# Attention and maxout FFN on one core: the ninth key blocks of four heads in 64x64 tiles of the array, 114 tiles masked on VectorE, the order of the work made anew

## The chip, the core and the metric

One core of a Trainium2 chip runs the whole program. Its engines work side by side, each through its own queue in order: TensorE (PE, with its weight loads shown apart as PEld), VectorE (DVE), ScalarE (ACT), GpSimd (POOL) and SyncE (SP), which here issues nearly all transfers. The metric is the time of one execution on the device, in microseconds; lower is better.

## The reference

Eight batches of eight heads, 576 positions of 64 numbers each. Attention keeps only scores within tau of the row's largest; its output goes through a feed-forward net with three parallel layers.

```python
scores = scale * np.matmul(q, k.transpose(0, 1, 3, 2))
thresh = np.max(scores, axis=-1, keepdims=True) - tau
scores = np.where(scores >= thresh, scores, -1000000000.0)
...
attn = attn / (np.sum(attn, axis=-1, keepdims=True) + 1e-09)
attn_out = np.matmul(attn, v)
...
h = np.maximum(np.maximum(x @ w1, x @ w2), x @ w3)      # x: 4608 x 512, w: 512 x 768
return h @ w_out                                        # 768 x 512
```

## The kernel before

**Tiling.** Four heads of one batch are a quad; there are 16 quads, two to a batch. The 576 positions are 9 blocks of 64 per head; two heads share the 128 partitions, so that a quad has two pairs of heads, r = 0 and 1 below. A chunk is 128 query rows of a quad, a tile is a chunk's scores for one r, 128 x 576 in fp32. A quad has 9 chunks and 18 tiles; there are 288 tiles.

**One tile.** `scores` (L287) makes it on TensorE in fp32 in a PSUM slot of two banks; there are four slots (SLOTS). The matmuls work in halves of the array: 64 rows x 128 columns (64\*128 in the profile's rows), and the ninth query chunk in four 64x64 tiles (64\*64). `maximum` (L319) takes the row maximum on VectorE. Then there are two ways, by a string of 288 digits, MASKED (L24), read by `masked` (L311). A tile with 0: ScalarE subtracts and flattens (`exponents`, L331, Prelu out of PSUM), then takes the exponential and its row sum (`numerators`, L339). A tile with 1: VectorE writes the negated scores to SBUF with the maximum, ScalarE takes one exponential, VectorE compares with the threshold, multiplies and sums in one instruction (SCALAR_TENSOR_TENSOR). So a masked tile uses ScalarE once and VectorE twice, one that isn't uses ScalarE twice and VectorE once.

After both tiles of a chunk, VectorE takes reciprocals (`reciprocals`), GpSimd scales to bf16 (`normalized`, tile P), and a transfer on SyncE's queue transposes P into `ptq` (`turned`).

**The product with V.** `product` (L366) multiplies a pair of heads' transposed probabilities by V in bf16 with 128 rows and 64 columns of the array (128\*64), two column tiles at once for the two heads of the pair. The 576 keys are four blocks of 128 and a ninth one of 64. The ninth blocks of the two pairs share one 128-row slot of `ptq` (index 4), pair 0 in rows 0 to 63 and pair 1 in rows 64 to 127. V for it is padded: three tiles `vr` are zeroed once in the other pair's rows (memsets, L553), and `cast_v` copies the 64 rows of each pair in, one GpSimd instruction for each. So the ninth block takes a whole pass of 128 rows for each product, of which half are zeros. The result is copied out of PSUM to `xt` by VectorE for pair 0 (`on_vector`) and by ScalarE for pair 1 (`on_scalar`).

**FFN.** `ffn` (L432): 18 hidden pieces (`hid`) a batch on TensorE, combined by ScalarE (copy, `hm`) and VectorE (two maxima), then output pieces (`outp`, `ninth`), copied out by ScalarE and stored. The last batch is split in two parts (SPLIT) of 256 and 320 positions, so that its first part can be worked on earlier.

**The order.** Every engine runs its instructions in the order of one string, ORDER (L40): each letter issues one step, and `_Ordered` (L82) chains each engine's instructions in that order. S, T, O, F, B are steps of TensorE (scores, transposes of q and k, products, first and second halves of FFN pieces; the digit names the PSUM slot); m, k, r, c, v, w are VectorE's; e, n, a, h, u, x ScalarE's; p, q, y, z GpSimd's (scaling, swapped copies of q, casts of V, casts of weights); l, t, g, o SyncE's transfers (loads, transposes of P, weights, stores). An engine doesn't step over an instruction that waits.

Of the kernel before, what the change touches and what calls it, by code (L numbers as in the profile page):

```python
# [12 lines left out]
BF16 = mybir.dt.bfloat16  # L13
# [11 lines left out]
010100101001000000011101001010000001100010001000101000011000100000100000  # L25
000011111001100001001001001001000001011100101001000110001010010000010011
000010011101100001001100100001001010001100010111000001000100000110000101
001001001101100000110001000100100100001100100011100111010011010111110110
# [12 lines left out]
lllllmlyelgS2ymylS3emgnlT0mleS1lakS2nlqermS3ylmeS0pmeS1kpS3elmS2nlzmelrmnT1pS0tcnperkT1pameS1zmteS3knpS0rnmp  # L41
emS2permeqS1mnqT3meqktepS0ncS2ntrpmS3npretprmeS1pmnS0tpmS3npmS1etpmeS0rT2mnplkeT1akgeS2qmgepmteS3rkpekntS0pe
rrnmT2pncS3ptamepS1meqtrS2meyqnS3lmqeS0pmelpknT1lpS2nmeymeS3lrkepS0tcnT2rpnmS1tpnmaprrmS0eS2pmteS1pmT3epctep
meT3O0ykntnyS2etrykpnO1wnprmaS0xptrS3meS2zmeS1mzgeS0mlnS3pmleS1pmelO2qmelpkteO0nrnklpS3nlwgxprrmS2leS0pmeF3q
tmT1eBqcF0eqkthBpnS2vS1nF3pmnF0pmBerBkepS2vhT1tnprmS0S3apmetS1zmeS2rmpeF3tmF0epBkepF1tnBvBznvS2ghS3rymnF0gmS
1eplBrkepF2tnmF3BnpvBnqvT1S0hprrcT2S3pamS1eymzF2emBeqgkF0etyS3nS1vpnmtF2pBmezBveS3prgnS0mtS1phrmT3epO2metzeF
0wpnS1gcqS2nmBqnmO3zekepgS1xvlF2nS3mtnF0rrmpBeBlpveS1lphS2mntF3zmeBrpS0evS1lpnmF2lnpS3rmleBptmS1nzvS0nS3mtpn
S2rpeF1rmepmtepS0mBepmtekF3ektekT2uBarklpukS0uqlS2urS1mlnS3pmleO0pmlepmelO2wtnkS1xrS0tepmF2myF3eBkepT1tBhcF0
nqvT2T1laByrcynS3qvS2nlqmF1tnpF0meS3pBelmBlhrrF2kpelS1vnBlprF3mnlS0pveBtprmS1hS2pmeS3tpmeS0pmF2emF1eBkeT3Bva
tF0nvqT2T3BkqlaS1nrcS3phmtS2npmF0epF1mteBqkBeqF3lnvS2lnBrvplS0hmtpS1F3meS2mteBrmepS0vnpO1rekpnO3mtnpweS2yrrt  # L50
xS1mF0yymT3epBcnS1pvS2nptF3meS0pmeBomT2hS1okeF0omF3ntBkaBervS1ponrF2vpemS0ptuS3mpeF2metknT1T3rknBparrceS0puS
3mqtuS1mpeS2mpeS3lmF0peomepS1ketqT3S2ncBqnmlqnmlO3ekluktO1urnwperrS0pxS3mptnS2mS1pempS3etmF0peF2meBlkBelS1kh
oF3nrmlF0pnBtvpBerrvS2phlS1mnpS3tmF0peS2mpeBmeF3vF1eoBkntS0vnBS2rmhpS3mepS1mteyF2mF0eyBkteBnrvT3pF1aovT2ynBp
lrcS3hplS0mnyF2lmF1elBykepBlnvT3tS0aS2vnO3rrmtpnmpeS1weptS2mS0prmO3eqtmeqF1eqlT0S2xqcBnlpmS3hlpS0meF2ymF1elB
knlF3vnBokBetS2hvS0nrrF3mpF1mpeBkBpetF2vnprS0uvnT3ptmS2aS1pmeS0trmF3epmnpkeS2tS0ermpBnmopnkS1uS2rurompS0eF3o
mpelmpeS2lkpeS0lmS1elqBmelqmetkO2unktO0erwpurkpT1txT2cS3apF0nmtT1qS2ceBqmnS1yF3hmF2eyrBpeBvptnF0pS1vnBrmtpS3
hS2pmeS0mtS1eF3meF2meBkBeF0knF1vnBBrvhpS3nvT0pF2akyF1tnBmyS0velByrmlS3phS2rlempF1lmyeF0pklBepS3tnvS2nBrmptO1
meprvepS2wnS3plmF0nF1rmepBlkeqS2lBhmtT3nyS0vnS2mqlO1emtpecT2xT0rS3pacF1eqmF2lnyBklqeT0BvlaS3khoS1qnmF0tF2pme
BrBopnvS3teprvF0pnrmS1puS2meS3prmS0epF1tmepmepT2ktBeqncT3tuS0kaS2urqmS3tnpmS1nF0pmemteS3repS1mS2lepmBelykteS
3kuO1rumplnmlpO0ewterpT2xS1cqnoS3mpF0nF2metBkeBkF1hlF3nvBlnrrS0pvlnBpmS2lhS1ymleF0mtS3epBmepF2vF1etkBnS0vnS3  # L60
rmBnpS2rhmpF0emF1pteBkpBerF3vnS2ptvnT0pBramS1pthS0mepF3meqtT2rBecpS1nvylT0ynS2pmlS3amlS1eomS0elO2rmpeomeplO3
ketnwT1F0nctF2xkBnBrvpS1hrF3pmS0qBemqS2onvF1yeF0mBopkeF3tyBnS2vqhBrlrnmpT1S0vaptS2empF1S3mpelBkeplF0vntS2rum
S1pnS0mtepF3rmepmetqS2kS0epBnmmteS1rkepS2lmuS0ulpmS1nlymT3yetF2cekeT3oBrknpamoS0npS3mnS1qtmuO0qurrmqelO2wpel
kpelS0xS3meptF2mS1peBemytF0hrkT3pBecF2nS1vpnS3rymtBpnmS0epS1vlnF3mF2etBmeBkhF0lkeF3nBrvpS1nrvBpnS2mptS0hmpeS
3meF2tmF1eBkeBlrvnT0plS3ravlpS2nlmqF0nlS1mqeBtrrmpF2eS3phBlmepS0tvepS1mS2npS3mepO0meknO1meownT3orxkT2pS0tacF
1nF2qrmeBtpS3evpBmS0tyhF1meT2yBcqoeF3rpkT2F0aptBnvBnS2pvS1hqtmF3nqT0meBrS1npvF2npmT3BactS1ervF3prmS0pueS2omp
F3ekqelmT1ntS0qcnBpmekteS2S1urrmpF0uompekS3eptS2nmS1pnmlO3ermtpekO2pnwS1ykxtyS3emS2BomeyrmepS1rukpS2uoF3meF0
opmnBtykBhpS1ervS2eptmO3pO0mxnS3txS2rmepF0empF1ekBtBevF3hkS2nS0mnBrmF1npF2vepBkBtS0hvO3emO2xkS1xerS3rpmF2mpF
0eF1kpteBnBvpF3BvtBrhkpF2S0vS1prmBptmF3eF0pveBtBhS1vS2mS3mF0F1mBkBF2vhF3keBeO0vnO1kF2kxeBwurS1rvpS0mpS2F3mpe
tmpeS0eoF1mnketBknkBurrupoF2puF0hptF3uvF2pvF1hF0tvF3rvpF2hF1vopF0vF3thF2vF1vF0hoF3vF2ovF1hF0vF3vO2uoO1wF0xF3  # L70
F2hF1vF3vF2hF1vF3vF2hF1vF3vF2hF1vF3vF2hF1vF3vF2hF1vBvF3uuooBF2uuuooo
# [31 lines left out]
def kernel(  # L103
# [609 lines left out]
    x = 0  # L713
# [39 lines left out]
```

## Time and profile before

| | us |
|---|---|
| timed runs, median of 3 | 447.21 |
| lowest and highest | 446.19, 447.46 |
| profiled execution, first to last instruction (span) | 445.0 |
| transposes of P, 144 on SyncE's queue, median to landing | 4.1 |
| loads of V, 32 of 256 KB, median to landing | 5.1 |

The profile shows one execution. Its page has busy times of each engine, busy tenths in 40 slices, the chain of work that ended last, and groups of instructions. All of the kernel's instructions are recorded at line 91, in the helper that keeps the order, so that they are told apart by the names of their tiles: sc are scores, o products with V, ph hidden pieces, po output pieces, tp transposes. A matmul's duration includes the time that it takes to run through, and the next one begins before it ends; so starts are compared, not durations. An fp32 matmul shows as two passes. TensorE ran at its full granted clock from 60 us on (mean 0.94 before that).

### The profile page before, as it was taken

To read this page: it belongs to the slowest core of one execution; us is meant where nothing else is said; L and a number is where in the kernel's file an instruction comes from. 1 tells how busy PE (TensorE), PEld (TensorE's weight loads), DVE (VectorE), ACT (ScalarE), POOL (GpSimd) and SP (SyncE) were. 2 spreads that over 40 slices of the span, in tenths; PEclk is the share of its full clock that TensorE was granted. 3 is DMA by queue.
4 is the path that set the end of the run, shared out by engine and by line. 5 is a ranking of instruction groups with operands and counts; after the bars stand their busy time and mean duration, and the time that the engine had idled before them with its cause. 6 is when DMAs were issued, how large, how long until landed. Compare 5 with 4: busy or idle time off the path is not lost.

```text
span 445.0 us, 14089 instructions
## 1 busy us (share of the span) xinstructions
PE 423.6 (95%) x5193; PEld 313.3 (70%) x5193; DVE 393.2 (88%) x1093; ACT 394.4 (89%) x804; POOL 315.9 (71%) x422
## 2 busy tenths in 40 slices
PE   7767799999999999999999999999999999999995
PEld 5434557767787767777687867867687778777772
DVE  4989889999999999989989998999999999989641
ACT  4999999999999999999998999999999999956422
POOL 3998989989686686686768885859767789562300
PEclk9998899999999999999999999999999999999999
DMA  8989999999999978999797999899999979882902
GB/s 251 331 162 213 243 195 234 221 245 229 215 255 195 250 165 175 234 187 228 179 223 170 200 224 182 211 234 199 197 220 202 253 121 173 148 122 34 217 13 108
DMA packets 212773, 87.44 MB, mean 196 GB/s; under 512 B 185824, under 2 KB 199648, under 8 KB 212704
## 3 DMA queue, kind: packets, MB, share of 16 engines
q1 hardware_dynamic: 212000, 85.69, 93.6%
q10 hardware_dynamic: 704, 0.85, 0.6%
q8 instruction: 41, 0.67, 0.6%
q14 instruction: 28, 0.23, 0.2%
HBM read 34.60 MB, written 9.44 MB: 99 GB/s over the span
## 4 chain that ended last, share of the span: by engine, by line
PE 81%; ACT 7%; DVE 6%; issue 4%; POOL 2%; DMA 1%; DVEq 0%; POOLq 0%; ACTq 0%
PE ph L91 30%; PE sc L91 28%; PE po L91 11%; PE o L91 8%; ACT z L91 6%; PE tp L91 4%; DVE z L91 2%; DVE unused L91 2%; DMA qm<-in_q_dram 1%; POOL P L91 1%; DVE hm L91 0%; POOL w L91 0%; ACT qt L91 0%; POOL qs L91 0%; DVE hT L91 0%
## 5 line engine op out<-in xcount | busy, mean ns | idle before, releaser
L91 POOL TENSOR_SCALAR P<-z,rs 128x576 bf16<-128x576 f32 x288 | 228.1, 807 | 85.7 <-DVE rs L91 36.4
L91 PE MATMUL sc<-kt,qt 64*128 64x320 f32 (+2 forms) x640 | 179.1, 429 | 4.9 <-ACT z L91 4.4
L91 PE MATMUL sc<-kt,qs 64*128 64x256 f32 (+2 forms) x640 | 178.6, 418 | 4.7 <-ACT z L91 2.7
L91 PE MATMUL ph<-xt,w 64*128 64x288 bf16 (+2 forms) x2160 | 163.9, 283 | 0.3
L91 PEld LDWEIGHTS <-w 64*128 64x128 bf16 (+1 forms) x2160 | 124.8, 94 | 30.9 <-issue 5.3
L91 DVE TENSOR_SCALAR_CACHE_REDUCE unused<-sc 128x576 bf16<-128x576 f32 x183 | 133.2, 749 | 8.9 <-PE sc L91 8.4
L91 ACT ACTIVATE z<-sc,nm 128x576 f32<-128x576 f32 x183 | 131.3, 740 | 8.5 <-DVE unused L91 5.2
L91 ACT ACTIVATE z<-z 128x576 f32<-128x576 f32 x183 | 123.5, 680 | 0.1
L91 PEld LDWEIGHTS sc<-kt,qs 64*128 64x128 f32 (+1 forms) x640 | 92.4, 178 | 25.3 <-ACT z L91 8.1
L91 PEld LDWEIGHTS sc<-kt,qt 64*128 64x128 f32 (+1 forms) x640 | 92.4, 178 | 19.8 <-ACT z L91 9.3
L91 DVE SCALAR_TENSOR_TENSOR z<-z 128x576 f32<-128x576 f32 x105 | 84.1, 811 | 0.4 <-ACT z L91 0.4
L91 DVE TENSOR_SCALAR_CACHE_REDUCE z<-sc 128x576 f32<-128x576 f32 x105 | 77.7, 752 | 7.4 <-PE sc L91 3.4
L91 ACT ACTIVATE z<-z,nm 128x576 f32<-128x576 f32 x105 | 79.1, 773 | 3.6 <-DVE z L91 3.2
L91 POOL COPY qs<-qt 64x640 f32<-64x640 f32 (+3 forms) x68 | 47.0, 692 | 14.4 <-ACT qt L91 11.0
L91 PE MATMUL po<-wo,hT 64*128 64x512 bf16 (+1 forms) x480 | 54.0, 356 | 0.1
L91 DVE TENSOR_TENSOR hm<-ph,hm 128x576 bf16<-128x576 f32 (+2 forms) x54 | 37.0, 686 | 13.0 <-PE ph L91 11.8
L91 ACT ACTIVATE hm<-ph 128x576 bf16<-128x576 f32 (+2 forms) x54 | 32.1, 594 | 18.4 <-PE ph L91 18.1
L91 PEld LDWEIGHTS <-hT 64*128 64x128 bf16 (+1 forms) x480 | 29.6, 97 | 17.1 <-issue 2.9
L91 DVE TENSOR_TENSOR hT<-ph,hm 128x576 bf16<-128x576 f32 (+2 forms) x54 | 37.2, 688 | 3.1 <-PE ph L91 0.6
L91 PE MATMUL o<-ptq,vb 128*64 128x64 bf16 (+2 forms) x544 | 38.7, 282 | 0.0
L91 ACT ACTIVATION_READ_ACCUMULATOR z<-z 128x1 f32 x183 | 36.2, 198 | 0.0
L91 PEld LDWEIGHTS <-vb 128*64 128x64 bf16 x544 | 22.6, 111 | 15.1 <-issue 6.8
(32 smaller groups left out, 274.2 us busy)
## 6 DMA issues: line engine op xcount, KB each, us to landing
vm<-in_v_dram SPq DMA_DIRECT2D x32, 256.0 KB, 5.1
out_dram<-ob SPq DMA_DIRECT2D x31, 256.0 KB, 2.8
qm<-in_q_dram SPq DMA_DIRECT2D x15, 512.0 KB, 4.5
km<-in_k_dram SPq DMA_DIRECT2D x15, 512.0 KB, 5.4
stage<-in_moe_w_dram SPq DMA_DIRECT2D x9, 512.0 KB, 5.3
ptq<-P SPq DMA_TRANSPOSE x144, 4.1
stage<-in_moe_w_out_dram SPq DMA_DIRECT2D x3, 512.0 KB, 4.7
qm<-in_q_dram SPq DMA_DIRECT2D x16, 64.0 KB, 2.9
```

What stands on the lines that cost most here:

```text
L91: ins = fn(*a, **kw)
```

## The change

- The ninth key blocks leave `product`, which now has four blocks. A new step N follows every second product: for both pairs of heads of the quad, the ninth block is multiplied with 64 rows and 64 columns of the array (`ninths`), pair 0 in the upper rows, pair 1 in the lower, two heads each in columns, and added to what the two products left in PSUM. The copies to `xt` (w, x) can be issued only after N.
- V for the ninth block is no longer padded: the six memsets go, the three fixed tiles are replaced by a pool tile `vrb` of 128 rows, and one GpSimd copy takes the place of two.
- In the last batch's second part the product's columns now lie at 256 to 575 of the bank, not at 0 to 319, so that each part lies in a bank as the others do.
- MASKED is new, with 114 ones in place of 105.
- ORDER is new throughout. It has the same steps, plus 18 N, less 16 y; and 9 k stand in place of 9 n.

```diff
 MASKED = """
-010100101001000000011101001010000001100010001000101000011000100000100000
...
+001110001001001001001000011110010001100000110110001001100000100001100001
...
 ORDER = """
-lllllmlyelgS2ymylS3emgnlT0mleS1lakS2nlqermS3ylmeS0pmeS1kpS3elmS2nlzmelrmnT1pS0tcnperkT1pameS1zmteS3knpS0rnmp
...
+S2ymlmS3lS1lelgllllllmlmlmS0T3mneeknamT2T1S3reeqaS1pqekmkS0enmrS3mcmpnreneS0S2merypenpmS1qnzkS3ppS2pmtS0geeT1
...
-    vrs = [one.tile([128, 4, D], BF16, name=f"vr{x}") for x in range(3)]
...
-        L["vrb"] = vrs[(2 * L["b"] + L["qd"]) % 3]
-        for r in range(2):
-            rows = slice(64 * r, 64 * r + 64)
-            pool.tensor_copy(out=L["vrb"][rows, 2 * r:2 * r + 2], in_=L["vr"][rows])
-            yield
+        L["vrb"] = vp.tile([128, 2, D], BF16, name="vrb")
+        pool.tensor_copy(out=L["vrb"], in_=L["vr"])
+        yield
...
-        order = [(m, run) for m in range(5) for run in runs] if part is None else \
-            [(m, run) for run in runs for m in range(5)]
+        order = [(m, run) for m in range(4) for run in runs] if part is None else \
+            [(m, run) for run in runs for m in range(4)]
...
-                    w = vb[:, 2 * r + i, (1, 3, 0, 2)[m], :] if m < 4 else vrb[:, 2 * r + i, :]
-                    tensor.matmul(ps[64 * i:64 * i + 64, p0:p0 + n], w,
-                                  pt[:, 4 if m == 4 else m + 5 * r, q0[i]:q0[i] + n],
-                                  start=(m == 0), stop=(m == 4))
+                    tensor.matmul(ps[64 * i:64 * i + 64, p0:p0 + n], vb[:, 2 * r + i, (1, 3, 0, 2)[m], :],
+                                  pt[:, m + 5 * r, q0[i]:q0[i] + n], start=(m == 0), stop=False)
+
+        def ninths(run):
+            *q0, p0, n = run
+            rows = slice(64 * r, 64 * r + 64)
+            for i in range(2):
+                tensor.matmul(st["ps"][64 * i:64 * i + 64, p0:p0 + n], vrb[rows, i, :],
+                              pt[rows, 4, q0[i]:q0[i] + n], start=False, stop=True)
...
-    for t in vrs:
-        for x in range(2):
-            vector.memset(t[64 - 64 * x:128 - 64 * x, 2 * x:2 * x + 2, :], 0.0)
...
             p.first(where)
-            for k, fn in (("x", p.scalar), ("w", p.vector)):
-                if fn:
-                    line[k].append(fn)
+            line["N"].append(p)
+        elif what == "N":
+            both = [line["N"].pop(0) for _ in range(2)]
+            for run in both[0].runs:
+                for p in both:
+                    p.ninths(run)
+            for p in both:
+                for k, fn in (("x", p.scalar), ("w", p.vector)):
+                    if fn:
+                        line[k].append(fn)
```

More of the change, by code (lines that the diff above doesn't have):

```diff
@@ L46 @@
[L46 to L60, printed above, removed]
@@ L392, in on_vector @@
             else:
-                vector.tensor_copy(out=dst[:, 256:S], in_=ps[:, 0:320])
+                vector.tensor_copy(out=dst[:, 256:S], in_=ps[:, 256:S])
         def on_scalar():
@@ L402, in on_scalar @@
             else:
-                scalar.activation(out=dst[:, 256:S], in_=ps[:, 0:320], func=AF.Copy)
+                scalar.activation(out=dst[:, 256:S], in_=ps[:, 256:S], func=AF.Copy)
         p = _Piece((L["b"], L["qd"], r, part), first)
@@ L406, in product @@
         p.scalar = on_scalar if part == 1 or r == 1 else None
+        p.runs, p.ninths = runs, ninths
         return p
@@ L595 @@
                 O=products(), F=pieces())
-    line = {k: [] for k in "menkrptahvuxwcq"}
+    line = {k: [] for k in "menkrptahvuxwcqN"}
     casts = iter([w[1] for w in wl])
```

54 lines of the change are left out of this document (35 added, 19 removed).

## The prediction

> **What bounds the kernel now.** I read the page first, its busy line and the chain that ended last.
>
> ```profile
> PE 423.6 (95%) x5193; PEld 313.3 (70%) x5193; DVE 393.2 (88%) x1093; ACT 394.4 (89%) x804; POOL 315.9 (71%) x422
> ...
> PE 81%; ACT 7%; DVE 6%; issue 4%; POOL 2%; DMA 1%; DVEq 0%; POOLq 0%; ACTq 0%
> ```
>
> TensorE carries 81% of the chain; VectorE and ScalarE share 13%. Whole-run shares hide stages, so next came busy time in four stretches, and one slice of 50 us.
>
> ```profile
> core 0: us, PE busy (x) PEld busy (x) DVE busy (x) ACT busy (x) POOL busy (x), PEclk, DMA share, GB/s
> 0.00:60.00 60.00, 43.82 (x389) 28.33 (x393) 48.25 (x145) 52.84 (x110) 49.66 (x72) 0.94 1.04 234
> 60.00:355.00 295.00, 294.30 (x3787) 220.47 (x3780) 278.81 (x772) 284.72 (x579) 226.17 (x301) 1.00 1.04 212
> 355.00:441.00 86.00, 85.53 (x1028) 64.51 (x1024) 66.06 (x178) 56.85 (x116) 40.07 (x51) 1.00 0.62 117
> ```
>
> ```profile
> 200.00:250.00 50.00, 50.00 (x650) 37.89 (x646) 48.06 (x133) 47.47 (x97) 36.47 (x49) 1.00 0.93 194
> ```
>
> Columns: stretch, length, busy us of each engine. Three stages show. Up to 60 us the feed-forward work has hardly begun, TensorE has gaps (43.8 of 60), and ScalarE is fullest (52.8). From 60 to 355 TensorE is busy throughout, yet ScalarE (284.7/295 = 96.5%) and VectorE (94.5%) are nearly as full: a three-way tie. From 355 to 441 only TensorE is full; what is left there is matrix work. Who holds whom in the tie is in the view of waits:
>
> ```profile
> PEld sc L91 <- ACT z L91: 17.3, 31, 2.2
> ...
> DVE unused L91 <- PE sc L91: 8.4, 20, 1.0
> ...
> ACT z L91 <- DVE unused L91: 5.2, 15, 0.7
> ...
> PE tp L91 <- DMA qm<-in_q_dram: 1.1, 2, 0.8
> ```
>
> (us in total, times, longest.) TensorE's score products, first of all their weight loads, wait for ScalarE to release PSUM banks, VectorE's maxima wait for those products, ScalarE waits for the maxima: a ring in which no member waits long. Work taken from TensorE counts fully only after 355, and before that as far as the other two keep up.
>
> **The ninth block.** TensorE around a pair of attention products, by start times (start, duration):
>
> ```profile
> 115.82 0.43 PE L91 MATMUL sc<-kt,qs 64*128 64x320 f32 x1
> 116.18 1.18 PE L91 MATMUL o<-ptq,vb 128*64 128x512 bf16 x16
> 117.19 0.41 PE L91 MATMUL o<-ptq,vr 128*64 128x512 bf16 x4
> 117.44 1.16 PE L91 MATMUL o<-ptq,vb 128*64 128x512 bf16 x16
> 118.43 0.41 PE L91 MATMUL o<-ptq,vr 128*64 128x512 bf16 x4
> 118.78 0.53 PE L91 MATMUL sc<-kt,qt 64*128 64x320 f32 x1
> ...
> 119.15 0.43 PE L91 MATMUL sc<-kt,qt 64*128 64x320 f32 x1
> ...
> 119.42 0.38 PE L91 MATMUL sc<-kt,qt 64*128 64x256 f32 x1
> ...
> 119.63 0.38 PE L91 MATMUL sc<-kt,qt 64*128 64x256 f32 x1
> ```
>
> Durations overlap, so I count from start to start. Four key blocks take 118.43 - 117.44 = 0.99, the fifth (vr, half of it zeros) 117.44 - 117.19 = 0.25. Now the same for the split last batch, and how often each shape runs:
>
> ```profile
> 405.35 0.28 PE L91 MATMUL o<-ptq,vr 128*64 128x256 bf16 x2
> 405.46 0.29 PE L91 MATMUL o<-ptq,vb 128*64 128x64 bf16 x8
> 405.58 0.20 PE L91 MATMUL o<-ptq,vr 128*64 128x64 bf16 x2
> 405.61 0.28 PE L91 MATMUL po<-wo,hT 128*64 128x256 bf16 x2
> ```
>
> ```profile
> L91 PE MATMUL o<-ptq,vr 128*64 128x512 bf16 x56 | 11.4, 382 | 0.0
> ...
> L91 PE MATMUL o<-ptq,vr 128*64 128x64 bf16 x64 | 6.8, 193 | 0.0
> ...
> L91 PE MATMUL o<-ptq,vr 128*64 128x256 bf16 x16 | 2.2, 272 | 0.0
> ```
>
> Matmuls come in pairs: 28 passes of 512+64 columns at 0.25 = 7.0 us, 8 of 256 at 405.46 - 405.35 = 0.11 and 4 of 64 at 0.03, 1.0 together. The padded ninths cost 8.0 us of TensorE. In the change four 64x64 tiles take what two passes took, 4.0 us if all four run at once. That is what the ninth query block's scores already do:
>
> ```profile
> 106.95 0.49 PE L91 MATMUL sc<-kt,qt 64*64 64x320 f32 x2
> 107.20 0.38 PE L91 MATMUL sc<-kt,qs 64*64 64x256 f32 x2
> 107.27 0.58 PE L91 MATMUL sc<-kt,qt 64*64 64x320 f32 x4
> ...
> 107.75 0.38 PE L91 MATMUL sc<-kt,qs 64*64 64x256 f32 x2
> 108.07 0.39 PE L91 MATMUL po<-wo,hT 64*128 64x512 bf16 x2
> ```
>
> The second halves of the two row tiles begin at 107.20 and 107.27; one after the other they would lie a pass (0.21 to 0.27) apart. So four tiles do overlap, in fp32; in bf16 no row shows it. Bounds of the saving: 4.0 and 0; I take 4.0, the nearest row.
>
> **Its price: changes of tile shape.** The 320-column pass from 115.82 takes 119.42 - 119.15 = 0.27 and ends at 116.09; o begins at 116.18. Afterwards vr ends at 118.43 + 0.25 = 118.68; sc begins at 118.78. From 64x64 back, 107.75 + 0.21 (119.63 - 119.42) = 107.96, po at 108.07. Each change of shape leaves 0.09 to 0.11 empty. In the programs' order I count 94 changes before and 106 after: 18 new ones between the last product and its ninths, less 6 by the new order. 12 x 0.09 = 1.1. TensorE: -4.0 + 1.1 = **-2.9 us**.
>
> The step also holds PSUM longer. A product's bank is free for its copy after its fifth block today; now the first product's waits for the second's four blocks and the ninths, 0.99 + 0.09 + 0.25 = 1.3 us longer, 18 times. TensorE spends that time on those very products. It costs nothing while VectorE and ScalarE have scores in the other two banks, 18 x 1.3 = 23 if they never have. They nearly do (the waits above are 0.2 to 0.6 us each on average): I take +0.4. Behind the two late copies stand the next maxima and exponents on these engines.
>
> **Masks: 105 to 114.** A masked tile gets its threshold and sum on VectorE in place of ScalarE's second pass.
>
> ```profile
> 401.99 0.75 DVE L91 SCALAR_TENSOR_TENSOR z<-z 128x576 f32<-128x576 f32 x1
> ...
> 402.67 0.75 DVE L91 TENSOR_TENSOR hT<-ph,hm 128x576 bf16<-128x576 f32 x1
> ```
>
> ```profile
> 201.35 0.67 ACT L91 ACTIVATE z<-z 128x576 f32<-128x576 f32 x1
> ...
> 202.02 0.67 ACT L91 ACTIVATE z<-z 128x576 f32<-128x576 f32 x1
> ```
>
> VectorE pays 402.67 - 401.99 = 0.68 a tile, ScalarE saves 202.02 - 201.35 = 0.67; the other instructions of a tile keep their number. Counting the masks by quad: 17 to 21 in the first three (about the first 60 us), 68 to 75 in quads 3 to 13 (60 to 355), 20 to 18 in the last two.
> - First stage: VectorE 48.25 + 4 x 0.68 - 0.7 (the six memsets, row below) = 50.3, ScalarE 52.84 - 2.7 = 50.1. The fullest engine loses 2.5 us. Bounds: 0 if the loads and GpSimd (49.66) set the pace, -2.5 if ScalarE does. I take **-1.2**.
> - Middle: VectorE 278.81 + 4.8 = 283.6, ScalarE 284.72 - 4.7 = 280.0. VectorE becomes the fuller of the two, 96.1% of 295 against ScalarE's 96.5% today; inside a stretch shorter by 2.5 it would need 97.0%. Bounds: 0 if it follows, +2.5 if the middle stage keeps its length. I take **+1.5**, nearer to the second, since in no row is VectorE above 48.06/50 = 96.1%.
>
> **The rest.** V of the ninth block is cast in one 128-row copy in place of two.
>
> ```profile
> L91 POOL CAST vb<-vm 128x1024 bf16<-128x1024 f32 x16 | 16.6, 1036 | 0.5
> ...
> L91 POOL CAST vr<-vr 64x128 bf16<-64x128 f32 x32 | 13.1, 411 | 1.2
> ...
> L91 DVE MEMSET vr<- 64x64 uint32 x6 | 0.7, 112 | 1.1 <-PEq L734 0.8
> ```
>
> One copy for 128 rows lies between 0.41 and 1.04; at 0.41 GpSimd saves 16 x 0.41 = 6.6, at 1.04 it loses 3.5. It is 71% busy, and its wait for work hides either; only in the first stage would it show, at 0.4 for each of two or three copies. The memsets end at 1.7 us, before any score. The loads are the same transfers. In the start, quad 1's transposes now stand together after the sixth score tile in place of spread over eight more; the queue of loads ahead of them is q, k, then weights and V, as before. I count nothing for it, and keep 1 us either way for the range, about what transposes wait for a landing today (last row of the waits, 1.1).
>
> **The sum.** -2.9 + 0.4 - 1.2 + 1.5 = -2.2 on the span of 445.0: 442.8. The median of the timed runs lies 447.2 - 445.0 = 2.2 above this span, so I forecast **445.0** (-0.5%). Its own range: all good ends -2.9 - 2.5 - 1 gives 440.8, all bad ends -2.9 + 0.4 + 2.5 + 1 gives 448.2.
>
> **Rivals.**
> - *VectorE becomes the bound* (slower). Its middle work grows to 283.6; if the new order lets it run only at today's 94.5%, that stage takes 300.1, 5.1 longer; with -1.2 from the start and -0.3 from TensorE in the tail the time is about 450.8. It decides as soon as VectorE's share stays under 283.6/295 = 96.1%. For it: that share is reached in one slice alone, the order is all new, and VectorE, queued in order, cannot step over a late score tile. Against it: ScalarE runs at 96.5% with the same kind of queue.
>   By the Trainium skill, "Perfetto Trace Analysis", "Identifying the Most-Contended Engine", TensorE should be judged by its weight loads, not its matmul time. Here that is 70% against VectorE's 88%, so the rule would give TensorE's 2.9 no worth and make this rival the answer. The trace bears it out only in part: between 116.18 and 118.68 passes start without a gap while the weight loads are not full.
> - *The four tiles do not overlap in bf16.* Nothing saved, 1.1 for the changes of shape, 0.4 and 0.3 as above: 449.0. For: the new pass reads four streams in bf16, which no row has. Against: the fp32 rows.
> - *The copies come too late.* If half of the 23 us of longer bank holds were exposed the loss would swamp all else, 455 and more; the short waits speak against it.
> - *A better order.* ScalarE and VectorE idle 10 and 16 of the middle's 295 us. If the new order fills 2 of ScalarE's 10 and VectorE follows, the +1.5 falls away too: -2.9 + 0.4 - 1.2 - 2 gives 441.5. For: GpSimd's lighter work in the start, where its output frees the z buffers. Against: transfers landing late cost the page's chain only 1%, so an order made for late landings has little to win.
>
> **Chances.** Forecast 0.40, VectorE 0.30, tiles 0.05, copies 0.05, better order 0.15, nothing moves (the terms cancel, 447) 0.05. A difference under 0.3% (1.3 us) cannot be told from none. The forecast's own range gives 0.30 faster, 0.07 the same, 0.03 slower; the better order is faster, the cancelling case the same, the other three slower, with a little of VectorE's low end (0.02) the same. Together: faster 0.45, same 0.14, slower 0.41. The range that leaves out the best and the worst tenth reaches from 440 to 454.
>
> **What would show it.** Ninths: rows of o with vr in 64*64, starts of the four within 0.1, and a pair of products plus ninths of 2 x 0.99 + 0.09 + 0.25 = 2.3 in place of 2.5. Shape changes: 0.09 before and after the ninths. Masks: VectorE busy 6 us more in total, ScalarE 6 less, and in 0 to 60 both near 50. If VectorE's share of the middle stage is below 96% while TensorE shows gaps before sc, the rival holds; if TensorE's middle share drops while the time does not, its saving was worth nothing. Wrong altogether: ninths that start one after another, or new waits of VectorE or ScalarE on o.

## The result and the profile after

| | us |
|---|---|
| changed kernel, median of 4 runs | 450.44 (448.77 to 451.40) |
| kernel before, median of 4 runs beside them | 446.70 (446.13 to 447.46) |
| ratio, 95% interval | 1.0082 (1.0055 to 1.0109) |
| profiled execution of the changed kernel, span | 446.9 |

The change makes the kernel 0.8% slower; forecast was 0.5% faster. Run again on another chip, the changed kernel stood at 1.0074 of the kernel before; below, a variant's gain is counted from the mean of the two, 1.0078, that is 3.5 us above the kernel before, with 446.7 us as the unit. The intervals of the ratios are about 0.2 to 0.3% either way, so that a gain counted like this is uncertain by about 1.2 us.

The busy line of the page and its chain that ended last, after the change:

```profile
PE 423.8 (95%) x5193; PEld 308.8 (69%) x5193; DVE 400.6 (90%) x1105; ACT 391.1 (88%) x786; POOL 318.9 (71%) x406
...
PE 76%; DVE 8%; POOL 5%; issue 5%; ACT 4%; DMA 2%; DVEq 0%; POOLq 0%
```

TensorE's part of the chain falls from 81% to 76%, those of VectorE and GpSimd rise, and the time doesn't fall. (In a second profile of the changed kernel TensorE's part is 49%, so little can rest on this share.) VectorE gained 7.4 us of work (6 forecast), ScalarE lost 3.3 (6 forecast), and GpSimd gained 3.0. The stretches of the prediction, after the change:

```profile
0.00:60.00 60.00, 45.64 (x381) 28.66 (x385) 48.73 (x142) 51.56 (x105) 50.11 (x68) 0.91 0.99 230
60.00:355.00 295.00, 291.55 (x3772) 215.73 (x3767) 285.35 (x789) 280.49 (x561) 228.52 (x289) 1.00 1.07 208
355.00:441.00 86.00, 85.44 (x1040) 64.11 (x1038) 66.27 (x177) 57.95 (x120) 40.31 (x51) 1.00 0.65 130
```

Fixed stretches compare different work once the kernels have drifted apart. So here are both kernels cut at the same steps: where the last product of quad 0, of quad 3 and of quad 13 ends, its ninths included, and at the end of the run (columns as in the prediction). First the kernel before, then the changed one:

```profile
0.00:58.00 58.00, 41.82 (x373) 26.91 (x373) 47.18 (x142) 51.31 (x107) 47.66 (x70) 0.94 1.03 234
58.00:118.60 60.60, 60.12 (x720) 43.08 (x718) 56.36 (x157) 59.18 (x122) 53.31 (x66) 1.00 1.08 229
118.60:372.90 254.30, 254.07 (x3302) 193.09 (x3298) 240.22 (x664) 244.08 (x497) 190.00 (x255) 1.00 1.01 204
372.90:445.00 72.10, 67.63 (x808) 50.23 (x804) 49.43 (x132) 39.84 (x79) 24.94 (x33) 1.00 0.57 111
```

```profile
0.00:56.50 56.50, 42.44 (x352) 27.16 (x355) 45.26 (x132) 48.53 (x98) 46.71 (x64) 0.91 0.99 236
56.50:121.30 64.80, 61.30 (x742) 43.31 (x736) 61.18 (x171) 61.00 (x125) 56.45 (x69) 1.00 1.12 223
121.30:372.50 251.20, 250.95 (x3290) 186.32 (x3286) 244.41 (x674) 239.54 (x480) 189.05 (x244) 1.00 1.06 203
372.50:446.90 74.40, 69.11 (x824) 52.02 (x816) 49.74 (x130) 42.01 (x86) 26.74 (x32) 0.99 0.53 117
```

Quad 0 is 1.5 us sooner, quads 1 to 3 take 4.2 us longer (64.8 for 60.6), quads 4 to 13 take 3.1 us less, the tail 2.3 us more: 1.9 in all, in the profiles. The middle, where the forecast saw the danger, gained. The early quads and the tail lost. (In the second profile of the changed kernel quad 3 ends at 121.2 and the tail takes 74.4, nearly the same; the middle takes 253.4 and gained only 0.9.)

Quads 1 to 3 cut finer, at the ends of the last products of quads 0, 1 and 2, before and after:

```profile
58.00:65.00 7.00, 6.96 (x78) 4.46 (x76) 5.97 (x18) 6.53 (x13) 5.56 (x8) 1.00 0.99 237
65.00:97.70 32.70, 32.32 (x412) 23.54 (x408) 30.75 (x83) 32.02 (x69) 31.14 (x39) 1.00 1.09 226
```

```profile
56.50:67.00 10.50, 9.08 (x106) 5.15 (x98) 10.08 (x32) 9.51 (x20) 10.00 (x13) 1.00 1.02 187
67.00:99.90 32.90, 31.65 (x416) 23.09 (x408) 32.10 (x82) 31.35 (x65) 29.55 (x37) 1.00 1.15 237
```

Quad 1 ends 2.0 us later than before, at 67.0 for 65.0, so most of the early loss of 2.7 has happened by then. TensorE, which was full in both stretches, now has gaps, and VectorE is busy for 96% and 98% of them (85% and 94% before). The granted clock (the third number from the end) is 1.00 in all four rows. What TensorE and VectorE wait for in quads 1 to 3, one row before and three after:

```profile
PEld sc L91 <- DVE z L91: 0.4, 2, 0.2
```

```profile
PEld sc L91 <- DVE z L91: 3.1, 4, 1.5
...
PE sc L91 <- DVE z L91: 1.5, 2, 1.0
...
DVE z L91 <- POOL P L91: 1.1, 2, 0.6
```

TensorE's score products now wait for VectorE there.

The ninths, by start times:

```profile
197.29 2.17 PE L91 MATMUL o<-ptq,vb 128*64 128x512 bf16 x32
199.39 0.44 PE L91 MATMUL o<-ptq,vrb 64*64 64x512 bf16 x8
199.76 0.42 PE L91 MATMUL ph<-xt,w 64*128 64x288 bf16 x4
```

The eight ninths stand in one row: in the records behind it the four of 512 columns start between 199.389 and 199.399, the four of 64 between 199.629 and 199.639. So all four tiles run at once in bf16, the bound taken (4.0 us) and not the other (0). From 199.629, 0.03 for 64 columns gives 199.66, and the next shape begins 0.10 later. And the waits, whole run:

```profile
PEld sc L91 <- ACT z L91: 11.4, 26, 1.3
...
PEld sc L91 <- DVE z L91: 9.6, 16, 1.7
...
ACT xt L91 <- PE o L91: 4.2, 5, 2.2
...
DVE xt L91 <- PE o L91: 2.9, 4, 1.6
```

TensorE's waits on ScalarE for z fell from 17.3 us, those on VectorE rose from 4.9 to 9.6. The last two rows stood at 2.5 and 1.4 before: the copies of the products wait a little longer, on 9 occasions. No flood of new waits on o.

### The profile page after: what moved, and what is told of

Its sections match the earlier page's. It is cut to its first block, busy times and chain, and to the rows that moved or that the text cites. A ratio compares the mean times of both kernels' runs of the same rounds, so it can differ in the third digit from the quotient of the medians.

```text
span 446.9 us, 14067 instructions
## 1 busy us (share of the span) xinstructions
PE 423.8 (95%) x5193; PEld 308.8 (69%) x5193; DVE 400.6 (90%) x1105; ACT 391.1 (88%) x786; POOL 318.9 (71%) x406
## 4 chain that ended last, share of the span: by engine, by line
PE 76%; DVE 8%; POOL 5%; issue 5%; ACT 4%; DMA 2%; DVEq 0%; POOLq 0%
PE ph L91 29%; PE sc L91 27%; PE o L91 9%; PE po L91 8%; DVE z L91 4%; POOL P L91 4%; PE tp L91 3%; ACT z L91 3%; DVE unused L91 2%; DMA ptq<-P 1%; DMA qm<-in_q_dram 1%; DVE hm L91 0%; DVE hT L91 0%; ACT qt L91 0%; DVE kt L91 0%
## 5 line engine op out<-in xcount | busy, mean ns | idle before, releaser
L91 POOL TENSOR_SCALAR P<-z,rs 128x576 bf16<-128x576 f32 x288 | 237.3, 838 | 83.1 <-DVE rs L91 38.4
L91 PE MATMUL sc<-kt,qt 64*128 64x320 f32 (+2 forms) x640 | 184.9, 434 | 6.2 <-DVE z L91 2.6
L91 PE MATMUL sc<-kt,qs 64*128 64x256 f32 (+2 forms) x640 | 183.0, 422 | 4.5 <-ACT z L91 1.7
L91 PE MATMUL ph<-xt,w 64*128 64x288 bf16 (+2 forms) x2160 | 171.1, 283 | 0.9 <-ACT z L91 0.4
L91 DVE TENSOR_SCALAR_CACHE_REDUCE unused<-sc 128x576 bf16<-128x576 f32 x174 | 127.9, 749 | 6.9 <-PE sc L91 6.3
L91 ACT ACTIVATE z<-sc,nm 128x576 f32<-128x576 f32 x174 | 125.8, 739 | 9.4 <-DVE unused L91 6.2
L91 ACT ACTIVATE z<-z 128x576 f32<-128x576 f32 x174 | 117.8, 680 | 0.6
L91 DVE SCALAR_TENSOR_TENSOR z<-z 128x576 f32<-128x576 f32 x114 | 94.8, 837 | 0.1
L91 DVE TENSOR_SCALAR_CACHE_REDUCE z<-sc 128x576 f32<-128x576 f32 x114 | 84.9, 750 | 8.3 <-POOL P L91 5.1
L91 ACT ACTIVATE z<-z,nm 128x576 f32<-128x576 f32 x114 | 86.5, 772 | 4.5 <-DVE z L91 4.2
```

What stands on the lines that cost most here:

```text
L91: ins = fn(*a, **kw)
```

## The experiments

Three causes could explain a loss with TensorE's saving in place: the copies that come later (the hold of PSUM banks), the nine more masks on VectorE, or the new order of the steps, whatever the masks. The runs take them one by one, then the first quads, where the profiles put the larger loss.

### Each half of the change alone

The ninths in 64x64 tiles in the old order, with the old 105 masks: N right behind the second product of 15 of the 18 pairs of products, and behind each product (a step M) in the other three, whose two products stand far apart; the copies right behind that.

```diff
-...epctepmeT3O0ykntnyS2etrykpnO1wnprmaS0xptr...
+...epctepmeT3O0ykntnyS2etrkpnO1NwnprmaS0xptr...
```

> The order and the 105 masks of before, with the ninth blocks in 64x64 tiles: 15 of the 18 pairs together behind their second product, three pairs (whose bank is used again in between) one product at a time; one cast of V fewer a quad. TensorE: passes saved 11 x 0.25 + 0.5 = -3.2 us, 115 changes of tile shape in place of 94 = +1.9, net -1.3. Theory 1 (TensorE's time counts, as predicted): 0.3% faster than before, near 445.5. Theory 2 (VectorE's nine more masked tiles made the change slow): the same as theory 1 here, since the masks are as before. Theory 3 (the longer hold of the banks makes it slow): slower than before by 1% or more. Theory 4 (the new order alone makes it slow): within 0.3% of before or faster.

453.31 us, ratio 1.0144 (1.0122 to 1.0166): 6.4 us slower, although TensorE has 3.2 us less to multiply; 21 more changes of shape, at 0.09 each, take 1.9 of that. The waits of that run:

```profile
DVE xt L91 <- PE o L91: 10.9, 13, 1.6
...
PEld sc L91 <- DVE xt L91: 6.5, 10, 1.1
...
PE sc L91 <- DVE xt L91: 2.2, 3, 0.9
```

VectorE, whose copy stands where the old order put it, now waits for the whole quad, 13 times; and the next scores wait for the bank that the copy frees.

The new order and its 114 masks alone, the ninths padded and inside the products as before (with the two casts of V's ninth block on GpSimd, and the memsets):

```diff
         elif what == "N":
             both = [line["N"].pop(0) for _ in range(2)]
-            for run in both[0].runs:
-                for p in both:
-                    p.ninths(run)
```

> The new order and the 114 masks, with the ninth blocks padded as before, inside each product; only the copies still wait for the second product. TensorE against the changed kernel: +4.0 us of passes, 89 changes of shape in place of 106 = -1.5, net +2.5. Theory 1 (TensorE counts everywhere): 2.5 us slower than the changed kernel, near 453. Theory 2 (VectorE is the bound in the middle): the middle stays and only the tail's part shows, +0.3 to +1, 450.5 to 451.5. Theory 3 (the hold of the banks, with the step between): the same or faster than the changed kernel. Theory 4 (the order): 451 to 453, as theory 1 or 2 but in any case 1% above before.

453.39 us, ratio 1.0136 (1.0114 to 1.0158). The order and masks alone cost 6.1 us, and putting the ninths into 64x64 tiles within that order gives 2.6 of them back (1.0136 to 1.0078). The order was made for the shorter products, so the 6.1 may hold a little that belongs to neither, and the 2.6 holds what the second cast and the memsets cost.

The changed kernel once more:

> The changed kernel as it is, for a time beside the other three on the same chip: 450.4, ratio to before 1.006 to 1.011.

450.13 us, ratio 1.0074 (1.0048 to 1.0101).

### The longer hold of the bank

The kernel before, multiplications untouched; only the first product's copy waits for the last matmul of the second, in 15 of the 18 pairs.

```diff
+                    def copy(fn=fn, n=n):
+                        ins = fn()
+                        if n % 2 == 0 and n // 2 not in APART:
+                            tc.add_manual_dep(ins.ins, products_done[n + 1].st["last"].ins.name, ...)
-                    line[k].append(fn)
+                    line[k].append(copy)
```

> The kernel before, padded ninths, its order and masks; only in 15 of the 18 pairs the copy of the first product now waits for the second product's last matmul as well, so its bank is held as long as with joint ninths. TensorE's work is that of before. Theory 'the hold of the first bank is what the joint ninths cost' (from the run with ninths in the order of before, 453.3): near that run, 451 to 454. Theory 'the 64x64 tiles and their changes of shape cost it': within 1 us of before.

453.88 us, ratio 1.0157 (1.0134 to 1.0179), with the waits of the run with the ninths alone:

```profile
DVE xt L92 <- PE o L92: 10.8, 12, 1.6
...
PEld sc L92 <- DVE xt L92: 6.4, 9, 1.1
```

So the hold by itself costs 7.0 us in an order that isn't made for it. The ninths alone, with nine of VectorE's 16 copies one to three of its steps later in the string:

```diff
-...S2etrkpnO1NwnprmaS0xptr...
+...S2etrkpnO1NnprmwaS0xptr...
```

> The run with the order of before and the ninths in 64x64 tiles, in which VectorE waited 10.9 us in 13 times for the products (1.4 in the kernel before). Here VectorE's copy of the first product stands behind one more of VectorE's steps in 10 of the 15 joint pairs, as far as the banks let it. Theory 'the copies come too late, and VectorE stands before them': VectorE's wait for o falls from 10.9 to 4 or less and the time from 453.3 by 3 to 6 us, to 447 to 450. Theory 'the banks are held too long, whoever copies': VectorE's wait falls, TensorE's waits for VectorE and ScalarE grow instead, and the time stays within 1.5 us of 453.3.

456.67 us, ratio 1.0217 (1.0192 to 1.0241), worse by 3.3.

```profile
PEld sc L91 <- DVE xt L91: 7.4, 10, 1.2
DVE xt L91 <- PE o L91: 6.0, 9, 1.6
PE sc L91 <- DVE xt L91: 5.5, 7, 2.0
```

VectorE stands less (6.0 for 10.9), but scores wait more for its copies (7.4 + 5.5 for 6.5 + 2.2): the late release is what is paid, not VectorE's standing.

In the changed kernel the ninths were moved ahead, between the two products, so that they end sooner after the first, at 18 more changes of shape.

```diff
-            p.first(where)
+            p.take(where)
...
+            if len(line["N"]) == 2:
+                for run in p.runs:
+                    for both in line["N"]:
+                        both.ninths(run)
+            p.first()
```

> The changed kernel with the ninths of both products between their other blocks: first product's four blocks, ninths, second product's four blocks. The first product is complete 1 us earlier, so its copy can go and its bank comes free earlier; changes of tile shape 124 in place of 106, +1.6 us of TensorE. Theory 'the hold of the first bank': waits of VectorE and ScalarE for o shrink from 7 us and the time falls by 1 to 4 us against the changed kernel (ratio to before 1.000 to 1.006). Theory 'the order itself, not the hold': +1 us from the changes of shape (ratio 1.010).

451.34 us, ratio 1.0110 (1.0082 to 1.0137): no gain. VectorE's wait for o falls from 2.9 us to 1.0, but the time doesn't fall. Even if the 18 changes of shape cost 18 x 0.09 = 1.6, the earlier release was worth nearly nothing: the new order leaves room for the hold.

### The masks beyond the first quads

The kernel before with nine tiles of quads 3 to 12 masked as well (n to k in place), 114 in all:

> The kernel before with nine more tiles of quads 1 to 12 masked (114), nothing else: VectorE +6.1 us, ScalarE -6.0. Theory 2 (nine more tiles on VectorE make it the bound): slower than before by 3 to 6 us, 450 to 453. Theory 4 (the order): within 1.5 us of before.

452.09 us, ratio 1.0119 (1.0096 to 1.0142): 5.3 us, 0.6 for each mask that the order wasn't made for. The changed kernel with five of its masks in quads 4 to 12 undone (k to n in place):

> The changed kernel with five of quads 4 to 12's masked tiles unmasked again (109 masks), their second step moved from VectorE to ScalarE at the same place. VectorE -3.4 us, ScalarE +3.3 in the middle stage, so both near 282 of 295. Theory 2 (VectorE is the bound): faster than the changed kernel by 2 to 3.4 us, 447 to 448.4. Theory 4 (the order): within 1 us of the changed kernel, 449.5 to 451.5, since the letters stand where they stood. Theory 1 says nothing of it.

452.52 us, ratio 1.0129 (1.0107 to 1.0152): slower by 2.3 still, which neither theory gave. In these two orders a tile moved either way, to VectorE or to ScalarE, cost about 0.5 us.

### What bounds quads 3 to 11

Three runs take work off one engine at a time in quads 3 to 11 of the changed kernel. One masked tile a quad compares 64 of its 576 columns (VectorE):

```diff
+            w = 64 if (number[g, idx], r) in FEW else S
-            vector.scalar_tensor_tensor(out=zn, in0=zn, scalar=thr, in1=zn,
+            vector.scalar_tensor_tensor(out=zn[:, :w], in0=zn[:, :w], scalar=thr if w == S else 0.0, in1=zn[:, :w],
```

> The changed kernel with less VectorE work: in one masked tile of each of quads 3 to 11 the compare, multiply and sum covers 64 of 576 columns and keeps all of them (so these tiles are not thresholded, and their sums cover 64 columns). VectorE -9 x 0.54 = -4.9 us, nothing added elsewhere. Theory 'VectorE is the bound in the middle': 4 to 5 us faster than the changed kernel, 445.5 to 446.5. Theory 'TensorE is': within 1 us of it, 449.5 to 451.5. Theory 'a ring of three': each engine gives back a part, 1 to 3 us, 447.5 to 449.5.

449.21 us, ratio 1.0050 (1.0030 to 1.0069): 1.3 us back, hardly more than the uncertainty. The same with the second exponential of one unmasked tile a quad (ScalarE):

> The changed kernel with less ScalarE work: in one unmasked tile of each of quads 3 to 11 the second exponential covers 64 of 576 columns (without the flattening; the other columns and the sum are not the reference's). ScalarE -9 x 0.43 = -3.9 us. Theory 'VectorE is the bound in the middle' and theory 'TensorE is': within 1 us of the changed kernel. Theory 'a ring of three': 1 to 2.5 us faster, 448 to 449.5.

451.38 us, ratio 1.0088 (1.0068 to 1.0108): nothing. One of the four key blocks left out of each product (TensorE):

```diff
+            few = 3 <= 2 * L["b"] + L["qd"] <= 11
...
+                if few and m == 3:
+                    continue
```

> The changed kernel with less TensorE work: in quads 3 to 11 the products leave out one of the four 128-key blocks (18 products x 0.25 = -4.5 us). Theory 'TensorE counts in the middle' (the predicted step): 3.5 to 4.5 us faster than the changed kernel, 446 to 447. Theory 'VectorE is the bound': within 1 us of it, 449.5 to 451.5. Theory 'a ring of three': 1 to 3 us faster.

447.70 us, ratio 1.0018 (1.0002 to 1.0034): 2.7 us for 4.5 of work. By the medians TensorE's time is worth most there, 0.6 for each us, VectorE's about a quarter, ScalarE's nothing; the first two lie where the expectations put a ring of three, so no single engine is shown to be the bound. The profiles don't place the gain: quads 4 to 13 take 251.0 us with TensorE's relief, 251.2 and 253.4 in the two profiles of the changed kernel.

### What bounds the first quads

The changed kernel, the same relief of VectorE, but in nine masked tiles of quads 0 to 3:

> The changed kernel with less VectorE work early: in nine masked tiles of quads 0 to 3 (two, three, two, two) the compare, multiply and sum covers 64 of 576 columns without threshold. VectorE -4.9 us in the first 120 us. Theory 'VectorE's five more masked tiles in the first four quads made it the bound there' (it was 97% busy between the products of quads 1 and 2): 3 to 5 us faster than the changed kernel. Theory 'the ring of three, no single bound': 1 to 2 us faster, as the same relief in quads 3 to 11 was.

446.06 us, ratio 0.9980 (0.9965 to 0.9995): 4.4 us back for 4.9 of work, over three times what the same relief gives later. Stretches of that run:

```profile
56.10:119.20 63.10, 60.12 (x740) 43.51 (x736) 58.63 (x168) 60.38 (x124) 53.14 (x68) 1.00 1.09 228
119.20:370.60 251.40, 250.91 (x3290) 186.36 (x3286) 244.36 (x674) 239.47 (x480) 188.68 (x244) 1.00 1.07 201
```

Quad 3's last product ends at 119.2 in place of 121.3, which places 2.1 of the 4.4 us; the profiled execution was the slowest of its twelve, and it doesn't place the rest. GpSimd has less to do as well, 45.35 + 53.14 = 98.5 us up to there for 46.71 + 56.45 = 103.2 (the section on the cost of an early mask says why). So the relief is VectorE's and GpSimd's together. For VectorE as the one that paces speak the waits above: TensorE waits for it, and it waits for GpSimd for 1.1 us only. The relief given to ScalarE, in nine unmasked tiles of the same quads:

> The changed kernel, with the second exponential of nine unmasked tiles of the first four quads made on 64 of their 576 columns (those tiles' results are left partly undone): about 3.9 us less of ScalarE up to the end of quad 3's product, VectorE and TensorE as in the changed kernel. Theory A: early it is VectorE, loaded by the 26 masks, that sets the pace. Then relief of ScalarE alone is worth 1 us at most: 449 to 451 us, ratio to the kernel before 1.005 to 1.010, and the length of quads 1 to 3 stays between 64 and 65.5. Theory B: early both engines pace together with the list, and any relief is worth as much as VectorE's (4.1 us): 446 to 447.5, ratio about 0.999, quads 1 to 3 at 63 or less.

449.81 us, ratio 1.0064 (1.0042 to 1.0085): 0.6 us, within the uncertainty; quads 1 to 3 took 63.9. And VectorE's relief in the kernel before:

> The kernel before, with the mask of nine masked tiles of the first four quads made on 64 of their 576 columns (those tiles' results are left partly undone): 4.9 us less of VectorE there, as in the run of the changed kernel with less of VectorE early. Theory A: the five masks that were added made VectorE the bound there. Then the kernel before, with 21 masks, gains less by the same relief than the changed kernel's 4.1 us: 0 to 1.5 us, 445 to 447 us, ratio 0.997 to 1.0. Theory B: VectorE was already the bound in the kernel before at that place. Then the gain is 3 to 4 us: 443 us, ratio 0.991 to 0.993, and the five masks are only part of a stage that cost time anyway.

445.75 us, ratio 0.9974 (0.9959 to 0.9989): 1.2 us, and quad 3's last product ends where it did (118.7 for 118.6). So VectorE as the bound of the first quads is new: the change made it so. Two masks of quad 1 undone, of tiles (13,0), which was masked before as well, and (15,1), which wasn't:

> The changed kernel with two of its early masks undone, of tiles (13,0) and (15,1) in quad 1 (112 masks, letters of the order changed in place): VectorE 1.1 us less there, ScalarE 1.0 us more. Theory A: VectorE paces the first quads, so about 0.8 us comes back: 449.5 us, ratio to the kernel before 1.006, and quads 1 to 3 take 63.5 to 64.5. Theory B: the order was made with these masks and is upset by any change of them, as by the five masks that were taken away further on: 450.5 to 452, ratio 1.009 to 1.013.

449.08 us, ratio 1.0041 (1.0022 to 1.0059): 1.7 us back for two masks, 0.8 each, in a place where undoing masks is as unplanned as it was further on, and there cost time. Quads 0 to 3 have 26 masks after the change and 21 before (quad 1 has seven in both); at 0.8 each the five would be some 4 us, an estimate from two masks whose 1.7 is itself uncertain by about 1.2.

### Old steps in the new order

The changed kernel with the first steps, up to the third quad's products, and their masks taken from the run with the ninths alone (both orders have issued the same work there but for two steps):

> The changed kernel with its order and masks up to the point where 80 of the 286 score steps and the first three quads' products are issued taken from the run in which the ninths alone were put into the old order (so 21 masks in the first four quads instead of 26, 110 in all; the ninths in 64x64 tiles throughout), and its own order from there on. Theory A: the loss sits in the early masks and their order, the rest of the new order stands by itself. Then quad 3's product ends near 119 us as in that run (57.3 + 61.8) instead of 121.3, quads 4 to 13 take 251 to 253, the tail 74.3: 448 to 448.5 us, ratio to the kernel before 1.003 to 1.005. Theory B: the early steps of the new order pay for what its middle gains (work done ahead). Then the middle grows by what the start gives: 450 to 451 us, ratio 1.007 or more, quads 4 to 13 at 254 or more.

449.24 us, ratio 1.0043 (1.0030 to 1.0057): 1.6 us back, and the middle kept its gain (252.0). The early steps don't pay for the middle. But quad 3's last product ends at 120.8, not near 119 as expected: quad 2's ends at 98.2 for 99.9, and quad 3, behind the seam, loses most of that again (22.6 us for 21.4). With the steps from quad 13's product on taken from there as well:

> As the run with the old start, and the order after the 250th score step (from before quad 13's product to the end) also taken from the run with the ninths alone in the old order, whose tail takes 73.5 us against 74.35 in the changed kernel; 112 masks. If the tail's loss belongs to the new order of its steps, 0.8 us more come back: 447.3 to 447.7 us, ratio 1.001 to 1.003, which would be level with the kernel before. If it is work that the middle left over, nothing comes back: 448 to 448.5.

450.94 us, ratio 1.0091 (1.0058 to 1.0124), seven runs from 448.1 to 454.3. The tail took 73.3 us for 74.3, but quads 4 to 13, which end at the second seam, took 257.6 in that profile, the slowest of the seven. So it doesn't settle whether 1 us of the tail's loss belongs to the new order of its steps or was work left over. Three other runs bear on the tail, which takes 72.1 us before and 74.4 after. In the old order the longer hold alone makes it 73.8 (the run in which the copy waits), nine more masks in earlier quads alone 72.2. In the changed kernel an earlier release (the ninths between the products) leaves it at 74.3.

### What an early mask costs

The groups of instructions up to quad 3's last product show why a mask costs more than 0.68 there. Kernel before, then changed kernel (xcount | busy, mean ns):

```profile
L91 POOL TENSOR_SCALAR P<-z,rs 128x576 bf16<-128x576 f32 x80 | 65.4, 832 | 7.6 <-DVE rs L91 5.4 <-issue 1.2
L91 DVE SCALAR_TENSOR_TENSOR z<-z 128x576 f32<-128x576 f32 x27 | 23.1, 870 | 0.4 <-ACT z L91 0.4
```

```profile
L91 POOL TENSOR_SCALAR P<-z,rs 128x576 bf16<-128x576 f32 x80 | 66.7, 848 | 8.8 <-DVE rs L91 3.7 <-ACT z L91 2.6 <-POOL vb L91 0.7
L91 DVE SCALAR_TENSOR_TENSOR z<-z 128x576 f32<-128x576 f32 x31 | 27.8, 901 | 0.1
L91 DVE TENSOR_SCALAR_CACHE_REDUCE z<-sc 128x576 f32<-128x576 f32 x32 | 23.8, 752 | 5.1 <-POOL P L91 3.5 <-PE sc L91 1.3
```

The maximum (last row) takes 752 ns, the mask of as many elements 901 on average, and 870 before. Counted one by one in the kernel before, the 38 masks during which GpSimd is idle take 742 to 756 ns, the 24 with GpSimd busy all along take 914 on average, from 747 to 1598. One of the longest of the changed kernel, first VectorE's timeline, then GpSimd's (start, duration):

```profile
88.52 1.63 DVE L91 SCALAR_TENSOR_TENSOR z<-z 128x576 f32<-128x576 f32 x1
```

```profile
87.08 1.47 POOL L91 TENSOR_SCALAR P<-z,rs 128x576 bf16<-128x576 f32 x2 [0.35 <-DVE rs L91]
88.50 1.04 POOL L91 CAST w<-stage 128x1024 bf16<-128x1024 f32 x1
89.60 1.02 POOL L91 COPY qs<-qt 64x512 f32<-64x512 f32 x1
```

A cast begins on GpSimd 0.02 us before the mask and ends at 89.54; the mask ends at 90.15, 0.61 after it, as if it had stood for most of the cast. By the Trainium skill, "SBUF — State Buffer", section "Who interferes with whom", a VectorE instruction with two inputs in SBUF contends with a GpSimd instruction that reads SBUF, and one with at most one input there, outside the two-port modes, doesn't. The mask reads z twice, the maximum reads PSUM. So the last run takes the second input away: the 26 masks of quads 0 to 3 read z once (the comparison times z is left out).

```diff
+            if number[g, idx] < 36:
+                vector.tensor_scalar(out=zn, in0=zn, scalar1=thr, scalar2=None,
+                                     op0=OP.max, op1=OP.add, accum_out=acc)
```

> The changed kernel, with the mask of the 26 masked tiles of the first four quads as an instruction of the same 128x576 on VectorE that reads z once (maximum with the threshold, and the sum) in place of twice (the comparison times z itself is left out). In the changed kernel the 31 masks up to the end of quad 3's product take 901 ns on average, and those with GpSimd idle 752. Theory A: the excess is a collision with GpSimd over the second operand. Then the new instruction takes 0.75 throughout, VectorE loses about 31 x 0.15 = 4.6 us up to quad 3's product, and as in the run with less of VectorE early 3 to 4 us come back: 446.3 to 447.5 us, ratio to the kernel before 0.999 to 1.002; GpSimd's scalings of P get shorter there as well. Theory B: the excess comes with the place, whatever the operands. Then it still averages about 0.9, and the time stays at 449.5 to 451, ratio about 1.0075.

445.73 us, ratio 0.9954 (0.9936 to 0.9972): 5.5 us back, more than either theory gave it. Its groups up to quad 3's last product, from the plain view and from the one that keeps shapes apart:

```profile
L91 POOL TENSOR_SCALAR P<-z,rs 128x576 bf16<-128x576 f32 x81 | 61.4, 770 | 15.9 <-DVE rs L91 8.9 <-issue 2.9 <-ACT z L91 1.2
```

```profile
L91 DVE TENSOR_SCALAR_CACHE_REDUCE z<-z 128x576 f32<-128x576 f32 x26 | 19.3, 744 | 0.5 <-ACT z L91 0.5
```

The new instruction takes 744 ns in the same places, and GpSimd's scaling of P falls from 848 to 770: 80 x 0.078 = 6.2 us of GpSimd, beside VectorE's 26 x 0.157 = 4.1. The excess belonged to the form with the second operand, and both engines paid it. The Trainium skill's rule, as the page and section above state it, agrees with these rows. Of the 5.5 us, VectorE's time explains most: the run with less of VectorE early took about as much off VectorE and gave 4.4, and the difference is within the uncertainty.

The collision isn't new: the early masks took 870 ns before. But more masks meet GpSimd more often, and over the whole run that shows on both engines. Before, then after, from the pages:

```profile
L91 POOL TENSOR_SCALAR P<-z,rs 128x576 bf16<-128x576 f32 x288 | 228.1, 807 | 85.7 <-DVE rs L91 36.4
L91 DVE SCALAR_TENSOR_TENSOR z<-z 128x576 f32<-128x576 f32 x105 | 84.1, 811 | 0.4 <-ACT z L91 0.4
```

```profile
L91 POOL TENSOR_SCALAR P<-z,rs 128x576 bf16<-128x576 f32 x288 | 237.3, 838 | 83.1 <-DVE rs L91 38.4
L91 DVE SCALAR_TENSOR_TENSOR z<-z 128x576 f32<-128x576 f32 x114 | 94.8, 837 | 0.1
```

Nine more masks take 10.7 us of VectorE, 1.2 each, and the scalings of P 9.2 us more of GpSimd. With nine more masks in the old order the scalings take 230.4, in the new order with padded ninths 237.1, so most of the 9.2 goes with the new order.

## Why the prediction went wrong, point by point

The forecast time was 445.0, the measured one is 450.4, 5.4 us off. The forecast span was 442.8, the measured one 446.9; the other 1.3 of the 5.4 us is mostly that the profiled execution was the fastest of the four (448.77 against a median of 450.44).

- **TensorE -2.9: right in its terms.** The passes halved, the four tiles overlap in bf16, a shape change costs 0.09 to 0.10, a pair with its ninths 199.66 - 197.29 = 2.37 (2.3 forecast). Within the new order the ninths gave 2.6 us (4.0 less 17 changes of shape is 2.5; the uncertainty is about 1.2). TensorE's busy time as a whole didn't fall (423.6 to 423.8): it fell by 3.1 in quads 4 to 13 and rose by 1.8 before and 1.5 after them. Ends of matmuls are modelled, so busy time also depends on what stands beside what. The rival of tiles that don't overlap is out.
- **Hold of PSUM +0.4: not contradicted here, but for a wrong reason.** It was read from short waits in the trace of before. In the order of before the hold costs 7.0, since its copies stand where a product used to end. In the changed kernel an earlier release gained nothing. The rival "copies come too late" (455) is near what the ninths alone gave in the old order (453.3, and 456.7 with the copies later).
- **First stage -1.2: the step that failed.** It was worked out from the fullest engine in 0 to 60 us, ScalarE, as if relief of ScalarE would shorten the stage, and with a range that excluded a loss (0 to -2.5). It should have asked for quads 1 to 3, and for which engine is late once tiles move: 3.9 us off ScalarE there gave 0.6, 4.9 off VectorE 4.4. Up to quad 3's last product the kernel lost 121.3 - 118.6 = 2.7 us, as VectorE's work there grew by 106.4 - 103.5 = 2.9; ScalarE's fell by 1.0 only. The forecast row, both engines near 50 in 0 to 60 us, came out at 48.7 and 51.6.
- **0.68 a mask: mis-sized in the same step.** The 0.68 was read at 402 us, where GpSimd was idle. Early, GpSimd is busy for 83 to 87% of the time (46.7 of 56.5 us, 56.5 of 64.8), and there a mask takes 0.15 more on average (901 - 752) and slows the scaling of P as well. Up to quad 3's last product four more masks took 27.8 - 23.1 = 4.7 us, 1.2 each; six memsets and one copy of a product left the stretch, so that VectorE's work grew by 2.9.
- **Middle +1.5: too high.** Ten of the eighteen pairs are in quads 4 to 13, 10/18 of TensorE's 2.9, or 1.6, so with the term they should have kept their length. They became shorter by 3.1 us in one profile and by 0.9 in the other, which puts the term between -1.5 and +0.7; its bounds were 0 and +2.5. VectorE was able to run at 244.41/251.2 = 97.3% there, above the 96.1% that the forecast had taken as its limit.
- **The rest 0: wrong by 2 us in the tail, and on GpSimd.** The tail took 2.3 more in both profiles; TensorE has more of its work left there (824 matmuls for 808) and more idle time. Why is open. GpSimd's one cast of V's ninth block took 0.32, under both bounds (0.41 and 1.04), which saved 7.9 us; yet GpSimd's work grew by 3.0, since the scalings of P took 9.2 more. The forecast had counted GpSimd's own instructions, not what VectorE's masks beside them do to their length.
- **Rivals.** "VectorE becomes the bound" gave 450.8 and the measurement is 450.4, but its place was wrong: it was to lose 5.1 in the middle with VectorE below 96.1%, and it didn't. VectorE did become the bound, but in the quads before that, so that the number fits by luck. The Trainium skill, "Perfetto Trace Analysis", "Identifying the Most-Contended Engine", named beside this rival, would have TensorE judged by its share of the peak rate (MFU) and its weight loads in place of matmul busy time; the prediction took the weight loads alone. By them (69% here, VectorE 90%) TensorE's time would be worth little, and by the medians that doesn't hold in the middle: 4.5 us off TensorE gave 2.7, 4.9 off VectorE 1.3, 3.9 off ScalarE none.

Not settled: how much of the early loss the order of the steps has beside the masks (the old start, which has the old masks too, gave back 1.6), how much of it is GpSimd's beside VectorE's, and the tail, which is nearly as large as the early loss. No variant that computes the whole reference beat the kernel before; the best stand at 449.1 and 449.2 us.

## What to carry to other kernels

Price an instruction at the place where it will run: a VectorE instruction with two SBUF operands costs what its neighbour on GpSimd makes of it, and GpSimd pays too. When work moves from one full engine to another, ask stage by stage which of them is late, and take small stages as seriously as the long one; a stage with a few us of slack on one engine loses it with a handful of moves. A step that lets a buffer go later is paid in the order, not in the step: the same hold cost 7 us in an order made without it, and in the order made with it an earlier release gained nothing.

## What the runs showed that was not expected

- Masks of the same size take 742 to 756 ns with GpSimd idle and up to 1629 beside it; a form that reads one operand from SBUF in place of two brought the early ones to 744 and the time down by 5.5 us.
- Four 64x64 tiles in bf16 begin within 0.01 us of each other, and the next four 0.24 after them.
- With the new order and its nine more masks on VectorE, GpSimd's scalings took 9.2 us longer, more than the 7.9 that the single cast of V's ninth block saved it.
- 4.9 us off VectorE were worth 4.4 in quads 0 to 3 of the changed kernel, 1.3 in quads 3 to 11, and 1.2 in quads 0 to 3 of the kernel before.
